# Reading a streamed weight half by even and odd partitions instead of by left and right columns

## The chip, the core and the metric

The kernel runs on one core of one Trainium2 chip. The metric is the device time of one execution in microseconds (us), and a smaller one is better. The engines are named as in the profile: PE multiplies matrices (PEld is its loading of weights), DVE, ACT and POOL work on vectors, SP issues transfers. A "q" behind an engine's name is its sequencer.

## The reference

The input x has 2048 rows of 640 numbers in bfloat16. Four layers follow each other, A, B, A, B, and each adds its result to what it gets:

```
x = x + A(layernorm(x));  x = x + B(layernorm(x))
x = x + A(layernorm(x));  x = x + B(layernorm(x))
```

A is attention over segments with a memory that goes from segment to segment. The rows are cut in 64 segments of 32. Each segment is put behind 8 memory rows, which gives 40 rows; these are projected to q, k and v for 32 heads of 192 (three matrices of 640 x 6144), attended with a mask that is causal except for the memory rows, and projected back (6144 x 640). The first 8 rows of the result are the memory of the next segment, the other 32 are the output. So the 64 segments can only be done one after the other.

B is local attention with 32 heads of 20: each row attends to itself and to the rows 2, 4, ... 14 places before it, between a projection to 1920 columns and one back to 640.

## The kernel before

One pass over the segments does all four layers. A step s handles segment s for the first A and, at the same time, segment s - 2 for the second A (LAG = 2), as two lanes l = 0 and 1 of one tile, so that each weight is used for both. It also does B for both lanes of the step before. There are 66 such steps and a last one with B alone. Each step needs the whole of the four weight matrices of A, and the new memory at its end is needed by its successor's first matmul.

**Weights.** A's weights are cut in 64 "halves" of [128 partitions, 1920 columns] bfloat16, 480 KB each: 0 to 31 for k and q (two for each pair of heads i), 32 to 47 for v, 48 to 63 for the output. 31 halves stay in SBUF (`RESIDENT`, tiles `res`). The other 33 (`STREAMED`) are read again in every step into a ring of five tiles `wt`. In step 0 a half is loaded from the matrices as they came, and POOL writes it in its SBUF form to a DRAM tile `Wr`; from step 1 on it is read from there, by two transfers on SP. `half(h)` does all this and is called by the three users of weights: `qk(i)` (L308, and L303 for i = 0), `v(i)` (L356) and `o(jh)` (L390).

**The step.** The order of a step is written out by hand in `ORDER`, four lines of words such as `q0 v0 q1 ...`. PE and SP keep exactly the order in which the program issues their instructions (`manual_schedule(engines={PE, SP})`). DVE, ACT and POOL are ordered by the scheduler of the framework, from times that it estimates, and it also puts in the waits. The last line of `ORDER` is

```
s3 pv2 wo0 o8 v13 v14 ln20 t3 v15 store0 o9 o10 pv3 o11 o12 o13 o14
```

Names that are used later, by line:

- `q` (qk): 30 matmuls `qk_ps<-ST,wt` or `res`, then ACT copies the result to `QK` (L310).
- `v`: 5 matmuls `v_ps` (L356), then a copy to `vt`, on ACT (L360) for even i and on DVE (L362) for odd i. `v15` is the last one.
- `s`, `t` (scores, p_transpose): matmuls L320 and L326, the softmax on DVE (L330 to L338) and ACT (L334, the exponential), the transpose L345, and its copies to `PT` on DVE (L347) and ACT (L348).
- `pv`: 24 matmuls `o_ps<-PT,vt` (L373), 6 for each of four `vt`; `pv3` uses v12 to v15. ACT copies the result to `ot` (L376).
- `o`: matmuls `acc<-ot,wt` or `res` (L390) that add up over the whole step in PSUM. `o14` does the halves 62 and 63.
- `finish_step`: DVE writes the new memory into `ST` of the next step (L401) and adds the residual (L414).
- B: `b_stats` (`ln10`), `b_qkv`, `b_logits`, `b_expand` (`e`), `b_wo`. Its layer norm uses POOL (L273), DVE (L275, L282 to L284, L291, L292) and ACT (L235, L236).
- `beta_x` (`ln20`): the layer norm of B's output on the same lines, but 32 columns wide; its L292 writes the second lane of the next step's `ST`.
- `input_load` and `input_tile`: every fourth step 128 new rows are loaded to `x_sb` (L241, on SP), normalised on DVE (L249 twice, L250, L252, L254) with two ACT instructions (L235, L236 on `lnst`), and transposed on PE (L259) a step later.
- `store`: every fourth step PE transposes 128 finished rows (L519) and ACT copies and stores them (L521, L522).

PSUM has six tiles (`ps`) that all these share in turn, and two more for `acc`.

Of the kernel before, what the change touches and what calls it, by code (L numbers as in the profile page):

```python
# [32 lines left out]
HALF = NCH * UW  # L33
# [73 lines left out]
class Kernel:  # L107
# [108 lines left out]
    def half(self, h):  # L216
        if h in self.resident:
            return self.resident[h]
        if h in RESIDENT:
            t = self.res.tile([P, HALF], BF16, name=f"res{h}")  # L220
            self.load_direct(t, h)
            self.resident[h] = t
            return t
        t = self.ring.tile([P, HALF], BF16, name="wt")
        if self.step == 0:
            self.load_direct(t, h)
            self.nc.gpsimd.dma_start(out=self.Wr[h][:, :], in_=t[:, :])
        else:
            for part in (slice(0, HALF // 2), slice(HALF // 2, HALF)):
                self.nc.sync.dma_start(out=t[:, part], in_=self.Wr[h][:, part])  # L230
        return t

    def rsqrt(self, var, out):
# [385 lines left out]
```

## Time and profile before

| | |
|---|---|
| time, median of 3 runs | 3518.95 us (3516.27 to 3520.65) |
| the profiled execution's own time | 3520.67 us |
| its span, first to last instruction | 3519.0 us |
| granted clock of PE, mean | 0.985 |
| PE busy | 3388.8 us, 96% |
| share of PE in the chain that ended last | 83% |
| DMA in that chain | 9% |
| read from HBM | 1091.68 MB, 316 GB/s with what is written |
| transfers `wt<-Wr` | 4290 of 240 KB, median 4.8 us from issue to landing |

A row of a group in the profile has the line, the engine, the operation, the tiles, the count, the busy time and the mean of one. A row of a wait names who waited and for whom, then the sum in us, how many times, and the longest. A row of a timeline has the start and the time taken in us, the engine, the line, the operation and its tiles, and in brackets the idle time of the engine ahead of it with what ended it. A row of a DMA queue has packets, MB and the time that its packets took, as a share of 16 engines' time. "issue" is a wait for which the profile shows no releaser.

### The profile page before, as it was taken

What the parts mean: (1) busy time and instruction counts of PE and PEld (TensorE: products, weight loads), DVE (VectorE), ACT (ScalarE), POOL (GpSimd) and SP (SyncE); (2) the same over time, 40 slices, a digit from 0 to 9 for tenths busy, and PEclk for the clock granted to TensorE, in tenths of its full rate; (3) what the DMA queues carried; (4) which work ended last, traced back from release to release, by engine and by line L of the source; (5) the groups of instructions that cost most, each with busy time, mean ns of one, the idle gap of its engine ahead of it and who ended that gap; (6) DMA issues with size and microseconds to landing.
All of it is one profiled execution on the core that took longest, in us unless ns stands there. A gap on an engine that the chain in (4) does not pass through costs nothing.

```text
span 3519.0 us, 172521 instructions
## 1 busy us (share of the span) xinstructions
PE 3388.8 (96%) x78044; PEld 2891.7 (82%) x78045; DVE 2197.2 (62%) x5056; ACT 1479.6 (42%) x3213; POOL 369.9 (11%) x467
## 2 busy tenths in 40 slices
PE   5799999999999999999999999999999999999997
PEld 3588888888888888888888888888888888888886
DVE  1366666666666666666666666666666666666665
ACT  1244444444444444444444444444444444444443
POOL 2110110010111011001101101110010111011000
PEclk7799999999999999999999999999999999999998
DMA  9999999999999999999999999999999999999995
GB/s 350 352 321 320 318 320 315 316 320 323 319 323 317 317 314 322 320 322 319 322 326 322 324 322 320 318 324 326 321 319 323 315 320 324 320 317 319 319 320 202
DMA packets 664961, 1121.84 MB, mean 319 GB/s; under 512 B 70744, under 2 KB 661472, under 8 KB 664224
## 3 DMA queue, kind: packets, MB, share of 16 engines
q1 hardware_dynamic: 659280, 1091.96, 92.5%
q0 software_dynamic: 2640, 16.22, 1.1%
q8 instruction: 610, 9.99, 1.1%
q10 hardware_dynamic: 2304, 2.62, 0.2%
q14 instruction: 127, 1.04, 0.1%
HBM read 1091.68 MB, written 18.84 MB: 316 GB/s over the span
## 4 chain that ended last, share of the span: by engine, by line
PE 83%; DMA 9%; DVE 4%; ACT 2%; SPq 1%; issue 1%; ACTq 0%; POOLq 0%; POOL 0%; DVEq 0%
PE qk_ps L308 29%; PE v_ps L356 21%; PE acc L390 13%; DMA wt<-Wr 4%; PE qkv_ps L438 4%; PE o_ps L373 3%; PE s_ps L326 3%; PE s_ps L320 3%; PE qk_ps L303 2%; PE bc_ps L480 2%; DMA x_sb<-in_A_x_dram 2%; PE pt_ps L345 1%; DMA wt<-in_A_Wv_dram 1%; SPq L214 1%; PE y_ps L492 1%
## 5 line engine op out<-in xcount | busy, mean ns | idle before, releaser
L310 ACT CAST QK<-qk_ps 128x480 bf16<-128x480 f32 x1056 | 581.5, 557 | 1042.7 <-PE qk_ps L308 828.5
L356 PE MATMUL v_ps<-wt,ST 128*128 128x384 bf16 x3630 | 717.4, 328 | 13.9 <-DMA wt<-in_A_Wv_dram 9.2
L308 PE MATMUL qk_ps<-ST,wt 128*128 128x80 bf16 x14850 | 687.8, 203 | 22.6 <-DMA wt<-in_A_Wq_dram 10.6
L308 PE MATMUL qk_ps<-ST,res 128*128 128x80 bf16 x14850 | 691.4, 202 | 18.1 <-DMA res<-in_A_Wq_dram 9.4
L308 PEld LDWEIGHTS <-wt 128*128 128x128 bf16 x14850 | 610.1, 100 | 78.8 <-DMA wt<-in_A_Wq_dram 11.8
L356 PEld LDWEIGHTS <-ST 128*128 128x128 bf16 x5280 | 466.1, 99 | 246.6 <-issue 16.4
L308 PEld LDWEIGHTS <-res 128*128 128x128 bf16 x14850 | 610.9, 100 | 48.9 <-DMA res<-in_A_Wq_dram 10.4
L390 PE MATMUL acc<-ot,res 128*128 128x80 bf16 x9900 | 465.6, 202 | 17.4 <-DMA res<-in_A_Wo_dram 9.6
L390 PEld LDWEIGHTS <-res 128*128 128x128 bf16 x9900 | 409.9, 100 | 38.3 <-DMA res<-in_A_Wo_dram 11.8
L362 DVE CAST vt<-v_ps 128x384 bf16<-128x384 f32 x528 | 290.2, 550 | 210.0 <-PE v_ps L356 209.8
L483 DVE TENSOR_TENSOR prod<-bc_ps,vh 128x512 bf16<-128x512 f32 x330 | 227.3, 689 | 245.0 <-PE bc_ps L480 244.4
L360 ACT CAST vt<-v_ps 128x384 bf16<-128x384 f32 x528 | 253.7, 481 | 244.8 <-PE v_ps L356 243.2
L485 DVE TENSOR_REDUCE oT<-prod 128x64 bf16<-128x512 bf16 x330 | 336.7, 1021 | 4.5
L356 PE MATMUL v_ps<-res,ST 128*128 128x384 bf16 x1650 | 326.8, 329 | 2.7 <-DMA res<-in_A_Wv_dram 2.7
L390 PE MATMUL acc<-ot,wt 128*128 128x80 bf16 x5940 | 309.9, 202 | 6.2 <-DMA wt<-in_A_Wo_dram 3.5
L376 ACT CAST ot<-o_ps 128x480 bf16<-128x480 f32 x528 | 268.4, 559 | 109.3 <-PE o_ps L373 109.3
L330 DVE TENSOR_TENSOR sb<-s_ps,maskA 128x320 f32<-128x320 f32 x264 | 129.7, 491 | 253.7 <-PE s_ps L326 253.6
L390 PEld LDWEIGHTS <-wt 128*128 128x128 bf16 x5940 | 261.3, 100 | 18.1 <-issue 4.7
L445 POOL TENSOR_TENSOR prod<-qT,kh 128x1280 bf16<-128x1280 bf16 x66 | 169.9, 2575 | 653.0 <-ACT kh L440 653.0
L348 ACT COPY PT<-pt_ps 64x320 bf16<-64x320 bf16 x264 | 110.9, 420 | 296.7 <-DVE PT L347 295.1
L273 POOL TENSOR_TENSOR sq<-x 128x160 f32<-128x160 bf16 x64 | 28.9, 452 | 1837.4 <-DVE x L496 1837.4
L445 DVE TENSOR_TENSOR prod<-qT,kh 128x1280 bf16<-128x1280 bf16 x66 | 201.2, 3048 | 3.4 <-ACT kh L440 3.4
(117 smaller groups left out, 3709.3 us busy)
## 6 DMA issues: line engine op xcount, KB each, us to landing
wt<-Wr SPq DMA_DIRECT2D x4290, 240.0 KB, 4.8
Wr<-wt POOLq DMA_DIRECT2D x33, 480.0 KB, 6.7
wt<-in_A_Wv_dram SPq DMA_DIRECT2D x11, 480.0 KB, 10.5
res<-in_A_Wo_dram SPq DMA_DIRECT2D x10, 480.0 KB, 10.8
wt<-in_A_Wk_dram SPq DMA_DIRECT2D x9, 480.0 KB, 11.1
res<-in_A_Wq_dram SPq DMA_DIRECT2D x9, 480.0 KB, 11.3
res<-in_A_Wk_dram SPq DMA_DIRECT2D x7, 480.0 KB, 10.2
wt<-in_A_Wq_dram SPq DMA_DIRECT2D x7, 480.0 KB, 10.2
```

What stands on the lines that cost most here:

```text
L308: nc.tensor.matmul(ps[:, m, :, :], lhsT=w[m // 3][:, c, (m % 3) * P:(m % 3 + 1) * P], rhs=st[:, c, :, 0:LT], start=(c == 0), stop=(c == NC ...
L310: nc.scalar.copy(out=self.QK[i % NQK][:, 0:12 * LT], in_=ps[:, :, :, :].rearrange("p m l t -> p (m l t)"))
L330: nc.vector.tensor_tensor(out=sb[:, :, :], in0=sv, in1=self.maskA[:, :].unsqueeze(1).to_broadcast([P, 8, LT]), op=ALU.add)
L356: nc.tensor.matmul(ps[:, :], lhsT=st[:, c, :, :].rearrange("p l t -> p (l t)"), rhs=w[:, c, :], start=(c == 0), stop=(c == NCH - 1))
L360: nc.scalar.copy(out=vt[:, :], in_=ps[:, :])
L362: nc.vector.tensor_copy(out=vt[:, :], in_=ps[:, :])
L376: nc.scalar.copy(out=ot[:, :, :, :], in_=ps[:, :, :, :, :].rearrange("p j n l t -> p (j n) l t"))
L390: nc.tensor.matmul(a[:, at, :, :], lhsT=w[h][:, m, dc * P:(dc + 1) * P], rhs=self.ots[h // 2][:, 3 * (h % 2) + m, :, :], start=(h == 0 and ...
L438: nc.tensor.matmul(ps[:, d, :, :], lhsT=self.wqkv[:, c, kind * D + d * P:kind * D + (d + 1) * P], rhs=self.xnB[:, c, :].rearrange("p (l t) ...
L445: eng.tensor_tensor(out=self.prod[:, :, l, :, :], in0=qT[:, :, l, :].unsqueeze(2).to_broadcast([P, NCH, BW, SEG]), in1=window(kh, l), op=A ...
L483: nc.vector.tensor_tensor(out=pv, in0=ps[:, :, :, :], in1=window1(self.vh, c), op=ALU.mult)
L485: nc.vector.tensor_reduce(out=self.oT[:, c, :].rearrange("p (l t) -> p l t", l=2), in_=pv.rearrange("p l w t -> p l t w"), op=ALU.add, axi ...
```

## The change

Only the two transfers of a streamed half change, from step 1 on. Before, the first one read columns 0 to 959 of all 128 partitions and the second columns 960 to 1919. After, the first one reads all 1920 columns of the partitions 0, 2, ... 126 and the second those of 1, 3, ... 127. Both forms move 240 KB per transfer, and the tiles in SBUF and in DRAM hold the same as before.

```diff
@@ -226,8 +226,8 @@
             self.load_direct(t, h)
             self.nc.gpsimd.dma_start(out=self.Wr[h][:, :], in_=t[:, :])
         else:
-            for part in (slice(0, HALF // 2), slice(HALF // 2, HALF)):
-                self.nc.sync.dma_start(out=t[:, part], in_=self.Wr[h][:, part])
+            for first in range(2):
+                self.nc.sync.dma_start(out=t[first::2, :], in_=self.Wr[h][first::2, :])
         return t
```

## The prediction

> **What bounds the kernel now.** I read the page first, then who waits for whom on PE over steps 1 to 64 (145.5 to 3438.5 us; a step lasts 51.4 us), then the end of a step on DVE, ACT and PE, and last the packets of the DMA queue.
>
> ```profile
> span 3519.0 us, 172521 instructions
> PE 3388.8 (96%) x78044; PEld 2891.7 (82%) x78045; DVE 2197.2 (62%) x5056; ACT 1479.6 (42%) x3213; POOL 369.9 (11%) x467
> ...
> q1 hardware_dynamic: 659280, 1091.96, 92.5%
> ...
> wt<-Wr SPq DMA_DIRECT2D x4290, 240.0 KB, 4.8
> ```
>
> PE is busy 96% of the span and SP's DMA queue (q1) 92.5%. Both are nearly full, so the question is which of them makes the other wait. PE's waits in steps 1 to 64 answer it:
>
> ```profile
> PE qk_ps L303 <- DVE ST L401: 14.4, 14, 1.8
> PE qk_ps L308 <- issue: 7.3, 16, 1.1
> PE acc L390 <- issue: 7.0, 8, 1.6
> PE qk_ps L308 <- DMA wt<-Wr: 6.9, 22, 0.5
> PE v_ps L356 <- issue: 3.4, 3, 1.5
> PE v_ps L356 <- DMA wt<-Wr: 1.0, 3, 0.5
> ```
>
> In 3293 us PE waits only 7.9 us (6.9 + 1.0) for streamed weights, the tile that the change touches. It waits 18.6 us for "issue" (these three lines and 0.9 in three small ones), where the profile shows no releaser, and 14.4 us for L401 on DVE. So PE sets the pace. The most that better transfers can give is 7.9 us, and 18.6 us more if the "issue" time is PE's instructions arriving late through the same full DMA engines (q8 moves 591 packets, 9.68 MB, in this stretch). That is 26.5 us, 0.75% of the time. 0.2% (7 us) is about what a measurement of this kernel can tell from no change.
>
> **The order on ACT and DVE changes too.** PE and SP are ordered by hand and POOL's order stays. On DVE and ACT the scheduler puts instructions by the times that it estimates, and in the changed program it decides otherwise at three places: the first and the third in nearly every step, the second in 14 steps.
>
> *First, DVE at the step's end, 64 steps.* The copy of v15 (L362) now stands behind L292 instead of ahead of it. DVE, then ACT, then PE before, in an ordinary step:
>
> ```profile
> 1019.22 0.31 DVE L347 COPY PT<-pt_ps 64x320 bf16<-64x320 bf16 x1
> 1019.48 0.56 DVE L362 CAST vt<-v_ps 128x384 bf16<-128x384 f32 x1
> 1020.39 0.33 DVE L292 TENSOR_TENSOR ST<-xc,ln_r 128x160 bf16<-128x160 f32 x1 [0.35 <-ACT ln_r L236]
> ```
> ```profile
> 1020.13 0.23 ACT L236 ACTIVATE ln_r<-ln_r 128x32 f32<-128x32 f32 x1
> ```
> ```profile
> 1020.47 0.62 PE L373 MATMUL o_ps<-PT,vt 128*64 128x80 bf16 x24
> ```
>
> L292 cannot start before 1020.39, since ACT's L236 releases it. The copy then starts 0.25 later (as L284 follows L291, which is as long as L292), at 1020.64, ends at 1021.20 and reaches PE 0.05 later (L401 to L303: 2205.86 to 2205.91). PE wants this vt for the last 6 of the 24 matmuls of pv3: 18 x 0.023 us after 1020.47, at 1020.88, or 0.1 earlier for its weight load. The stall is 0.37 to 0.47 us; I take 0.42. Behind it on PE stand o11 to o14 and the next step, nothing with slack. In the 16 steps with a store, PE transposes first and pv3 starts 0.34 after L292 (1071.54 against 1071.20), and o12 waits 0.3 us for ACT anyway: nothing there. So 48 x 0.42 = +20.2 us (bounds 48 x 0.30 = 14 and 48 x 0.56 = 27).
>
> *Second, DVE in the 14 steps in which an input tile arrives.* Before, all five layer-norm instructions of the tile stand ahead of L401, which makes the next step's state:
>
> ```profile
> 2203.38 0.89 DVE L249 BATCH_NORM_STATS2 bst<-x_sb 128x6 f32<-128x320 bf16 x2 [2.46 <-DMA x_sb<-in_A_x_dram]
> ...
> 2205.30 0.45 DVE L254 TENSOR_SCALAR xn<-x_sb,lnst 128x640 bf16<-128x640 bf16 x1
> 2205.66 0.20 DVE L401 CAST ST<-acc 128x48 bf16<-128x48 f32 x1
> ```
>
> L401 comes 2.28 us after x_sb has landed. After, one L249 (0.45) is left ahead of it and the others stand behind the six L401 and L414, so L401 comes 1.83 us sooner. The longest of the 14 stalls is 1.84: all of the 14.4 us goes (bound -10, if x_sb lands later). What is late next: ACT's L235 for the input now waits for L250, and q0's copy behind it moves from 1.3 to about 3.0 us after the step's start. PSUM's six tiles cover that: q0's is wanted again by q3, 5.2 us after the start.
>
> *Third, ACT.* L236 goes ahead of q2's copy (which moves by about 0.35 us), and the exponential L334 ahead of q4's copy (by 0.8 us, and qT and kh with it by 0.4 and 0.25). Those tiles are wanted over 2 us later by PE (lg at 17.2 us of the step, POOL's and DVE's products ending near 14). 0; without that cover up to 0.25 x 64 = 16 us.
>
> **The transfers.** 4290 transfers stay 4290, each 240 KB. Each had 128 rows of 1920 bytes and has 64 of 3840. Rows of 3840 bytes occur in the load of wqkv, 5 to 9 us; below it the steady stretch, 145 to 3438 us:
>
> ```profile
> q1 hardware_dynamic: 439, 1.69, 102.2%
> ```
> ```profile
> q1 hardware_dynamic: 610318, 1040.73, 94.0%
> ```
>
> 1.69 MB in 439 packets is 3840 bytes each: such a row goes as one packet, in 1.022 x 16 x 4 us / 439 = 149 ns. In the steady stretch it is 0.940 x 16 x 3293 us / 542,250 packets over 512 bytes = 91 ns for 1920 bytes. Two of those are 182 ns, so the engines' work falls by up to 18%, or not at all if a long row is stretched by a full queue as the short ones may be. The gain on PE lies between 0 and 26.5 us. I take -8, under a third, because the "issue" part is unproven and a wait is shortened rather than taken away.
>
> Two rules of the Trainium skill speak against the change. "SBUF — State Buffer", Door 1, says that a transfer's rate hangs on how many of 16 ports its partitions reach, 64 neighbouring ones reaching 8; by its formula the even partitions reach all 16. "DMA: Bandwidth & Descriptors", Rules for kernel authors, says not to split a transfer by partitions but to use all 128. No row here shows a transfer of every second partition; what halved ports would cost is a rival below.
>
> **PE's waits.** Before, a half's first weight load waits for the first transfer and a later one for the second. After, the first waits for both. An instruction carries one wait; a second is an EVENT_SEMAPHORE ahead of it. PE gets some 2145 of these (33 halves x 65 steps). Of that kind it has one per step now:
>
> ```profile
> L308 PEldq EVENT_SEMAPHORE  x65: 51/51/51, 168.3 to 3459.8; - x65
> ```
>
> One falls at 1044.78, inside a run of 30 matmuls of o that takes 1.07 us like those without it (1044.15 to 1045.22): the sequencer runs ahead, PE does not see it. 0, but where PE is already waiting for a transfer, the two matmuls that needed only the first one (2 x 0.036 us) start later: 25 waits x 0.07 = +2.
>
> **Sum.** The profiled execution took 3520.67 us. 3520.67 + 20.2 - 14.4 - 8 + 2 = 3520.5. That run lies 1.7 us over the median, 3518.95, so I say **3519 us**: no change that can be told.
>
> **Rivals.** *The copy of v15 decides (slower).* The place is pv3; it wins from the point at which the transfers give back less than 1 us: 3519 + 20.2 - 14.4 + 2 = 3527, and at 27 us for the copy 3534. For it: the order is fixed in the program and L292's release does not move. Against: the 14.4 us nearly pay for it. 0.22.
>
> *The transfers give all they can (faster).* All 26.5 us go: 3519 + 20.2 - 14.4 - 26.5 = 3498. For it: 149 against 182 ns; the stretch's DMA share of 0.96 leaves the queue little room today. Against: most of it is "issue". With half and more of it, 0.25.
>
> *PE pays for its new waits (slower).* If the 51 ns are exposed each time: 2145 x 0.051 = 109 us, 3628. Against it stand the 65 of today. 0.08.
>
> *Half the ports (slower).* If two engines share one port, a row takes 298 ns; a half's 8 rows per engine take 2.4 us, 33 of them 79 us, against the step of 51.4. The queue then sets the time: 65 x 27 us more, about 5300. 0.05. By what the Trainium skill's "SBUF — State Buffer", Door 1, says of 64 neighbouring partitions this would come; by its port formula it would not.
>
> That long rows are cut in two, so that nothing changes in the packets, is spoken against by the 439 packets; it would end in the first rival.
>
> **How the numbers follow.** No change: 0.40. Faster by over 0.2%: 0.25. Slower by over 0.2%: 0.22 + 0.08 + 0.05 = 0.35. The range reaches from the second rival (3498, and 1 for the low bound of the copy) to the first with its upper bound and the input's gain at 10 (3542): 3497 to 3542; the last two rivals are left out, 0.13, and a little at both ends.
>
> **What the profile after would show.** The packets of q1 fall by about 274,560 and its share below 92.5%. PE's waits for L401 are gone. PE or its weight load waits for DVE vt L362 at L373, about 48 times, some 0.4 us each. Waits for wt<-Wr and "issue" together fall below 26 us. EVENT_SEMAPHORE on PE counts about 2145, and runs of 30 matmuls still take 1.07 us. The prediction is wrong if L373's waits are missing (the copy has cover that I did not see), if wt<-Wr grows to several us per step (ports), or if PE's runs stretch (waits).

## The result and the profile after

The changed kernel takes **3710.78 us** (median, 3694.03 to 3725.71) against 3517.61 us before (3510.34 to 3520.65): ratio 1.0551, 95% interval 1.05 to 1.0602. It is 193 us slower; the prediction said 3519 us with a range of 3497 to 3542. The profiled execution of it took 3704.68 us. Its page:

```profile
span 3703.0 us, 174588 instructions
PE 3449.1 (93%) x78045; PEld 2916.6 (79%) x78045; DVE 2104.9 (57%) x5056; ACT 1504.4 (41%) x3213; POOL 364.8 (10%) x467
...
q1 hardware_dynamic: 384720, 1091.96, 86.8%
...
wt<-Wr SPq DMA_DIRECT2D x4290, 240.0 KB, 4.8
```

q1's packets have fallen by exactly 274,560 and its share fell from 92.5 to 86.8%: the DMA engines have more spare time than before, and still PE waits for weights. PE's waits in steps 1 to 64 (144.7 to 3621.7 us; total us, times, longest):

```profile
PE qk_ps L308 <- DMA wt<-Wr: 58.7, 75, 3.5
PE v_ps L356 <- DMA wt<-Wr: 38.3, 49, 2.2
PE qk_ps L308 <- issue: 16.3, 23, 2.0
PE acc L390 <- issue: 13.3, 17, 2.0
PE o_ps L373 <- DVE vt L362: 10.5, 42, 0.3
PE acc L390 <- DMA wt<-Wr: 7.2, 14, 1.3
```

The 64 steps take 3477.0 us instead of 3292.9, 184 more. With all lines of this view added up, waits for wt<-Wr went from 7.9 to 104.2 us, "issue" from 18.6 to 41.0, L401 from 14.4 to 0.7; L373's wait for the copy of v15 is new. Together PE's waits went from 42 to 168 us. Another 57 us stand in PE's busy time (3248 us before, 3305 after, in these steps). Much of that goes with the waits too: in a run a matmul starts every 0.036 us, but the last one ahead of a wait counts with its whole 0.2 us, and there are 259 waits where there were 72; that is 34 us. The weight loads (PEld) wait for the streamed tile as well, 57 times and 61 us, but 51 of these fall in time in which PE stands, and are counted above.

What has changed ahead of all this is SP. Its issue of one transfer, in ns min/median/max, in the kernel before and after:

```profile
L230 SPq DMA_DIRECT2D wt<-Wr x4290: 319/400/2304, 134.3 to 3482.7; - x195
```
```profile
L230 SPq DMA_DIRECT2D wt<-Wr x4290: 450/587/2552, 133.5 to 3666.9; - x195
```

And SP itself waits much longer for the output store, after and, below it, before:

```profile
SPq L230 <- DMA out_dram<-yo: 71.8, 15, 6.1
```
```profile
SPq L230 <- DMA out_dram<-yo: 4.2, 8, 0.9
```

**The slot's way round.** Each streamed half goes into one of five slots. For the 2046 halves of steps 2 to 63 the traces give the mean time of each leg: from the last matmul that read the slot's old half to the issue of the first new transfer; from there to the second transfer's issue (part of the next leg); from the first issue to the later landing; from there to the first matmul that reads it; the reading itself. The sum is what one slot takes for one half; times 33 halves over 5 slots it is the step. In us:

| kernel | free to issue | (1st to 2nd issue) | issue to landed | landed to use | use | step |
|---|---|---|---|---|---|---|
| before | 0.195 | (0.449) | 5.425 | 1.341 | 0.832 | 51.4 |
| after | 0.522 | (0.614) | 5.580 | 1.290 | 0.833 | 54.3 |

After, a slot waits 0.33 us longer for SP, and the half lands 0.155 us later. 0.48 x 33/5 x 64 = 203 us; the leg from landing to use is 0.05 us shorter, which takes back 21 us. The legs add up to the step by their definition, so this says where the time stands and not yet why.

### The profile page after: what moved, and what is told of

The parts are those of the page before. It is cut to its first block, busy times and chain, and to the rows that moved or that the text cites. A ratio compares the mean times of both kernels' runs of the same rounds, so it can differ in the third digit from the quotient of the medians.

```text
span 3703.0 us, 174588 instructions
## 1 busy us (share of the span) xinstructions
PE 3449.1 (93%) x78045; PEld 2916.6 (79%) x78045; DVE 2104.9 (57%) x5056; ACT 1504.4 (41%) x3213; POOL 364.8 (10%) x467
## 3 DMA queue, kind: packets, MB, share of 16 engines
q1 hardware_dynamic: 384720, 1091.96, 86.8%
## 4 chain that ended last, share of the span: by engine, by line
PE 67%; DMA 19%; DVE 7%; SPq 3%; issue 2%; ACT 2%; POOLq 0%; POOL 0%; ACTq 0%; DVEq 0%
PE qk_ps L308 23%; DMA wt<-Wr 16%; PE v_ps L356 16%; PE acc L390 12%; PE qkv_ps L438 3%; PE o_ps L373 2%; PE s_ps L326 2%; PE s_ps L320 2%; SPq L230 2%; PE qk_ps L303 2%; DMA wt<-in_A_Wv_dram 2%; PE bc_ps L480 2%; DVE vt L362 1%; PE pt_ps L345 1%; SPq L214 1%
## 5 line engine op out<-in xcount | busy, mean ns | idle before, releaser
L310 ACT CAST QK<-qk_ps 128x480 bf16<-128x480 f32 x1056 | 583.8, 555 | 1027.0 <-PE qk_ps L308 838.8
L308 PE MATMUL qk_ps<-ST,wt 128*128 128x80 bf16 x14850 | 699.0, 203 | 83.1 <-DMA wt<-Wr 58.7
L356 PE MATMUL v_ps<-wt,ST 128*128 128x384 bf16 x3630 | 718.8, 329 | 52.3 <-DMA wt<-Wr 38.8
L308 PEld LDWEIGHTS <-wt 128*128 128x128 bf16 x14850 | 616.3, 101 | 150.0 <-issue 65.3
L308 PE MATMUL qk_ps<-ST,res 128*128 128x80 bf16 x14850 | 694.4, 203 | 24.7 <-DMA res<-in_A_Wk_dram 8.4
L356 PEld LDWEIGHTS <-ST 128*128 128x128 bf16 x5280 | 465.9, 99 | 296.3 <-issue 51.6
L308 PEld LDWEIGHTS <-res 128*128 128x128 bf16 x14850 | 613.2, 101 | 56.9 <-DMA res<-in_A_Wk_dram 10.7
L390 PE MATMUL acc<-ot,res 128*128 128x80 bf16 x9900 | 467.0, 203 | 19.1 <-issue 11.2
L390 PEld LDWEIGHTS <-res 128*128 128x128 bf16 x9900 | 410.9, 100 | 40.0 <-issue 13.1
L356 PE MATMUL v_ps<-res,ST 128*128 128x384 bf16 x1650 | 328.7, 330 | 4.0 <-DMA res<-in_A_Wv_dram 2.3
L390 PE MATMUL acc<-ot,wt 128*128 128x80 bf16 x5940 | 309.2, 202 | 17.1 <-DMA wt<-Wr 7.2
L390 PEld LDWEIGHTS <-wt 128*128 128x128 bf16 x5940 | 258.7, 100 | 33.9 <-issue 16.2
L445 POOL TENSOR_TENSOR prod<-qT,kh 128x1280 bf16<-128x1280 bf16 x66 | 191.1, 2895 | 745.3 <-ACT kh L440 745.3
L334 ACT ACTIVATE sb<-sb 128x320 f32<-128x320 f32 x264 | 124.1, 470 | 192.2 <-DVE sb L333 192.0
```

What stands on the lines that cost most here:

```text
L308: nc.tensor.matmul(ps[:, m, :, :], lhsT=w[m // 3][:, c, (m % 3) * P:(m % 3 + 1) * P], rhs=st[:, c, :, 0:LT], start=(c == 0), stop=(c == NC ...
L310: nc.scalar.copy(out=self.QK[i % NQK][:, 0:12 * LT], in_=ps[:, :, :, :].rearrange("p m l t -> p (m l t)"))
L334: nc.scalar.activation(out=sb[:, :, :], in_=sb[:, :, :], func=ACT.Exp, scale=SCA)
L356: nc.tensor.matmul(ps[:, :], lhsT=st[:, c, :, :].rearrange("p l t -> p (l t)"), rhs=w[:, c, :], start=(c == 0), stop=(c == NCH - 1))
L390: nc.tensor.matmul(a[:, at, :, :], lhsT=w[h][:, m, dc * P:(dc + 1) * P], rhs=self.ots[h // 2][:, 3 * (h % 2) + m, :, :], start=(h == 0 and ...
L445: eng.tensor_tensor(out=self.prod[:, :, l, :, :], in0=qT[:, :, l, :].unsqueeze(2).to_broadcast([P, NCH, BW, SEG]), in1=window(kh, l), op=A ...
```

## The experiments

All ratios are to the kernel before, run on the same chip, where it took 3517 to 3522 us beside each experiment. First the transfer's form, with everything else as before.

**Partitions 0-63 and 64-127.** 
```
-            for part in (slice(0, HALF // 2), slice(HALF // 2, HALF)):
-                self.nc.sync.dma_start(out=t[:, part], in_=self.Wr[h][:, part])
+            for part in (slice(0, P // 2), slice(P // 2, P)):
+                self.nc.sync.dma_start(out=t[part, :], in_=self.Wr[h][part, :])
```


> Two transfers of whole rows again, but partitions 0-63 and 64-127 instead of even and odd; the order of instructions on DVE, ACT, POOL and SP is that of before, so neither the copy of v15 nor the 14 input steps play a part, and none of the lanes moves. PE's first weight load of a half still waits for both transfers. Four theories stand for the 186-193 us that the change cost. ISSUE (SP needs 450/587 ns, min/median, for a transfer of every second partition against 319/400, so slots are refilled later): here it depends on what makes the issue long; if it is the step over partitions, SP shows about 320/400 and the time is within 20 us of before; if it is the 64 rows of 3840 bytes, SP shows 450/587 and the time is 3518 + 100 to 140. FIRST WAIT (the first weight load needs both transfers): slower than before by 60 us or more with SP at 320/400. STORE (SP waits 72 us for the output store in 15 steps) and ORDER (copy of v15, +16 to 20): same as before, as neither is in this kernel. If engines share ports by partitions, the queue's share goes to 100% and the time to thousands of us more (5300 by the rival in the prediction).

Measured: 4692.97 us, 1.3323 (1.3285 to 1.3361). Its SP line and its queue:

```profile
L230 SPq DMA_DIRECT2D wt<-Wr x4290: 444/445/2135, 134.1 to 4656.2; - x195
```
```profile
q1 hardware_dynamic: 384720, 1091.96, 99.5%
```

The same 384,720 packets fill the queue: they cost 0.995 x 4692.7 / (0.868 x 3703.0) = 1.45 times the engine time of even and odd partitions. So the dearer packets, which the prediction held possible for the change itself as a sharing of ports, come with neighbouring partitions and not with every second one. The Trainium skill, "SBUF — State Buffer", Door 1, draws that line by its port formula, and these two shares agree with it. The long issue (444 ns at the least) is here too: it belongs to 64 partitions, not to the step of two.

**Column halves, second columns first.** 
```
-            for part in (slice(0, HALF // 2), slice(HALF // 2, HALF)):
+            for part in (slice(HALF // 2, HALF), slice(0, HALF // 2)):
```


> The two column halves of before (128 rows of 1920 bytes each), the second columns asked for first. Orders on all engines are those of before, SP's issue costs are those of before (319/400 ns). PE's first weight load now needs the transfer that is issued last, as after the change. FIRST WAIT: this alone makes PE late, 60 us or more over before, and wt<-Wr among PE's waits rises from 8 to over 60 us. ISSUE, STORE and ORDER: within 15 us of before, since a late half costs PE only the two or three matmuls that it could have run ahead (0.07 us for qk, 0.18 for o, 0.33 for v, where PE is waiting at all).

Measured: 3529.67 us, 1.0038 (1.0024 to 1.0051). PE's wait for both transfers costs 8 to 18 us by itself, far from 60.

**One transfer for each half.** 
```
+            w = self.Wr[h]
+            self.nc.sync.dma_start(out=t[:, :], in_=w[:, :])
```


> One transfer of 128 rows of 3840 bytes for each half; orders on DVE and ACT as before. SP issues 2145 transfers instead of 4290. ISSUE: SP's time for issues falls (one issue for each half, even at 600 ns it is 20 us a step against 31 before and 40 after), a half is complete earlier by one issue, so PE's waits for wt<-Wr stay near 8 us and the time is 3490 to 3525. FIRST WAIT: the first weight load waits for the whole half as after the change, so slower than before by 60 us or more. STORE, ORDER: as before.

Measured: 3604.91 us, 1.0243 (1.0225 to 1.026). Both expectations missed the way of it. SP's issue takes 319/320 ns, slots are refilled at once (0.03 us), but PE stands 67 us for "issue" (18.6 before) and only 15.5 for wt. Every one of its 54 "issue" gaps over 0.4 us ends 1.1 to 1.6 us after a 16 KB packet of the instruction queue (q8) has ended, where the mean distance of such packets is 5.7 us. I read this as PE's next instructions coming late through the same DMA engines. The Trainium skill, "DMA: Bandwidth & Descriptors", Rules for kernel authors, advises one transfer over 128 partitions in place of two partition halves. It is faster here than even and odd partitions (3605 against 3711), but two column halves are faster than both.

**The output store off SP's semaphores.** The edit is on the changed kernel:
```
-        nc.scalar.dma_start(out=self.out[...], in_=yo[:, :])
+        nc.gpsimd.dma_start(out=self.out[...], in_=yo[:, :])
```


> The changed kernel with one edit: POOL issues the output store instead of ACT, so that no transfer of SP follows it in its lane. Orders on DVE and ACT are those of the changed kernel. STORE: SP's 72 us of waits for out_dram vanish, the 15 steps that showed 56.5 us against 53.5 of their neighbours come down to 53.5, and the time falls by 40 to 50 us, to 3660-3670. ISSUE, FIRST WAIT, ORDER: what SP waits there is taken from waits that it would have had anyway, and the time stays within 10 us of the changed kernel's 3711.

Measured: 3657.98 us, 1.0407 (1.0374 to 1.044): 53 us come back. Why it costs so much shows in the trace of the changed kernel. The hardware transfers of SP and ACT take eight completion semaphores in turn, and a transfer waits for the one before it on its own. At 1115.39 us ACT issues the store, and SP's next transfer is the one behind it on that semaphore (ACT's and SP's instructions):

```profile
1115.39 0.34 ACTq L522 DMA_DIRECT2D out_dram<-yo  x1
```
```profile
1120.10 0.45 SPq L230 DMA_DIRECT2D wt<-Wr  x1
```

SP stands 4.7 us from the store's issue until it has landed, and the DMA engines run dry (their busy tenths, and GB/s, in 40 slices of 1115 to 1121 us):

```profile
DMA  7888999897966768997654331000000000300000
GB/s 307 358 333 358 333 333 333 333 333 307 365 256 256 282 265 316 367 376 256 273 205 171 128 111 60 34 26 17 17 26 9 0 0 0 109 0 0 0 0 0
```

It is so at all 15 stores of steps 1 to 64: the semaphore's next user is SP's first transfer behind the store. Before, it is the seventh, and SP waits 4.2 us for stores in all. The step after each store lasted 56.5 us in the changed kernel and lasts 53.6 here, as its neighbours do.

**Short rows again.** Both kernels get a gap of 64 bytes in DRAM between a row's column halves:
```
-            self.Wr = {h: self.dram.tile([P, HALF], ...
+            self.Wr = {h: self.dram.tile([P, 2, HALF // 2 + 32], ...
```


> The changed kernel with the cached weights laid out in DRAM with a gap of 64 bytes between the two column halves of a row, so that even and odd partitions still go as two transfers, but in packets of 1920 bytes (128 for each transfer) as before the change. Orders on all engines are those of the changed kernel. LONG ROWS (rows of 3840 bytes keep the DMA engines from PE's instruction fetches and cost the time that single transfers lost, 86 us): PE's waits for issue fall from 36 to 20 us or less and the time falls by 20 to 60 us, to 3650-3690. ISSUE (SP's time for a transfer of 64 partitions): no change within 15 us if SP shows 450/587 again; more if SP needs longer for 128 packets than for 64; if SP's time follows the form of the rows and comes out at 320/400, then back to 3580 or below.

> The single transfer for each half again (3605 us), with the same gap in DRAM, so that its 256 packets have 1920 bytes. Orders on DVE and ACT are those of before. LONG ROWS: PE's waits for issue fall from about 70 us to the 18 to 25 of before, and the time to 3520-3540. If it is the size of the transfer (480 KB in one go ahead of everything else) and not the length of its rows, it stays within 15 us of 3605.

Measured: 3707.0 us, 1.0535 (1.0515 to 1.0554), the same as the changed kernel; and 3580.06 us, 1.0167 (1.0151 to 1.0182), 25 below the single transfer but still 1.7% above before. So shorter rows by themselves gave the changed kernel nothing back. SP's line of the two:

```profile
L230 SPq DMA_DIRECT2D wt<-Wr x4290: 579/597/2287, 134.7 to 3665.9; - x195
```
```profile
L230 SPq DMA_DIRECT2D wt<-Wr x2145: 517/518/1659, 134.7 to 3541.1; - x195
```

Two packets to a row make the issue longer still, which muddies both: in the first, slots wait 0.69 us for SP, so that a gain from shorter rows could hide behind it.

**The scheduler's order, in the kernel before.** The copy of v15 behind L292; the input tile's layer norm behind the step's end:
```
+        elif i == 15 and 1 <= self.step <= self.n_seg:
+            with self.tc.issue_after(self.applied):      # L292
+                nc.vector.tensor_copy(out=vt[:, :], in_=ps[:, :])
```


> The kernel before with one thing pinned: the copy of v15 stands behind L292 on DVE in every step, as in the changed kernel; nothing else moves on any engine. ORDER (first term of the prediction): +20 us (14 to 27), 3533 to 3545. If pv3 has cover that the prediction did not see: within 5 us of before. If the ring of five slots takes the delay back (SP refills while PE stands): less than half, +2 to +10.

```
+                        with tc.issue_after(self.last_xr):   # the last L414
                             self.input_tile(s // 4 + 1)
```


> The kernel before with one thing pinned: the input tile's layer-norm instructions stand behind L401 and L414 of the step's end on DVE in the 14 steps that take an input tile; some ACT instructions move with them. Second term of the prediction: the 14.4 us of L401's stalls go, 3500 to 3508. If the time is set by the ring (slot released to landed) rather than by PE's own work, PE stands elsewhere instead and the gain is under 7 us.

Measured: 3537.34 us, 1.005 (1.0037 to 1.0063), +18; and 3510.49 us, 0.9974 (0.996 to 0.9987), -9. PE's wait of the first (lines stand three further down in this kernel):

```profile
PE o_ps L376 <- DVE vt L363: 13.1, 48, 0.3
```

48 times, as the prediction counted, but 0.27 us each where it had 0.42. In the second, waits for L401 are gone.

**SP busier, first try.** Four and eight empty instructions on SP behind each transfer of the kernel before:

```
                 self.nc.sync.dma_start(out=t[:, part], in_=self.Wr[h][:, part])
+                for _ in range(4):                           # or 8
+                    self.nc.sync.nop(nofuse=True)
```


> The kernel before with four empty instructions on SP behind each streamed transfer, so that SP is busy longer with each as it is after the change (147 ns more on the mean there: 40.4 against 30.7 us for the 66 transfers of a step). Rows, packets and all orders are those of before. How long four of them take will be read from the distance of SP's two transfers of a half (0.45 us on the mean before, 0.61 after the change); between 70 and 200 ns are possible. ISSUE: slower, in proportion; the two runs that showed the other parts leave 3711 - 3518 - 53 (store) - 17 (order) + 10 (input) - 12 (first wait) = about 120 us for 147 ns, so at that length 3600 to 3640, at 70 ns 3555 to 3575. If SP's time is hidden (it waits for slots 20 us of each step): within 10 us of before.

> The same with eight empty instructions: ISSUE says twice the loss of the run with four or more, since a busier SP has more slots waiting in line; hidden says nothing until SP is full, at 66 x 0.78 us = 51.4 us a step, which eight would only reach at 40 ns each.

Measured: 0.9994 (0.9981 to 1.0008) and 1.0003 (0.9992 to 1.0014). They say nothing: the instructions did not come to execution, SP has its 6581 instructions and the distance of 0.44 us as before.

**The changed kernel with store and order put right.** On top of the store on POOL, L292 is pinned behind the copy of v15 (excerpt):

```
-        self.ln_apply(self.x2_next[:, :, :], m, r, ...)      # L291 and L292 ahead of v15's copy
+        nc.vector.tensor_tensor(out=self.xc2[:, :, :], ...)  # L291 stays
+    def apply(self):                                         # a stage of its own, behind v15
+        with self.tc.issue_after(self.v15):
+            self.nc.vector.tensor_tensor(out=self.ST[...][:, :, 1, NM:LT], in0=self.xc2[:, :, :], ...)
```


> The changed kernel with the store issued by POOL (3658) and, besides, the copy of v15 pinned ahead of L292 on DVE, as it is before the change. ORDER: PE's 43 waits at L373 for vt go, and the time falls by the 16 us that the same order cost in the kernel before, to 3637-3647. If the ring sets the time in this kernel (a slot's release to its landing), PE's wait only moves into waits for wt: within 7 us of 3658.

Measured: 3650.09 us, 1.0381 (1.0357 to 1.0405). 8 us less than with the store alone, with intervals that overlap: not told apart. What it leaves is 3650 - 3530 = 120 us over the swapped column halves, with the copy of v15 in the same place and the same wait for both transfers. The input tile still stands behind the step's end here, which is worth 9 us, so the form of the transfers costs nearer 129.

**A slightly better kernel.** Before, with two of the edits above together (`issue_after(self.last_xr)` around the input tile, `nc.gpsimd.dma_start` for the store):

> The kernel before with the input tile's layer norm behind the step's end on DVE (3510) and the store issued by POOL. STORE as a fault of the changed kernel's timing alone: before waits only 4.2 us for out_dram, so 3505 to 3512. If the store on a lane of SP costs every kernel its waits: 3460 to 3490.

Measured: 3507.56 us, 0.997 (0.9958 to 0.9982): the input's gain, and nothing for the store. The store costs only where its place on the semaphores falls badly.

**SP busier, in earnest.** Semaphore increments, which do execute, behind each transfer of the kernel before (three, six), and three with the swapped columns:
```
                 self.nc.sync.dma_start(out=t[:, part], in_=self.Wr[h][:, part])
+                for _ in range(3):
+                    self.nc.sync.sem_inc(self.busy)
```


> The kernel before with three increments of an unused semaphore on SP behind each streamed transfer; rows, packets and all orders are those of before. One such instruction and the gap to the next take about 50 ns on SP by the traces (17 and some 33), so the distance of a half's two transfers goes from 0.45 to about 0.60 us, against 0.61 after the change. ISSUE: most of the 120 us that are open, 3590 to 3640. HIDDEN (SP waits for slots for 20 us of each step): within 15 us of before, and the 120 us belong to the form of the transfers (64 partitions of long rows), not to SP's time.

> The same with six increments: distance about 0.75 us, and SP busy for 66 x 0.75 = 49.5 us of a step of 51.4 by itself. ISSUE: more than twice the loss of the run with three, 3700 or over. HIDDEN: 3520 to 3600.

> Column halves with the second columns asked for first (3530 by itself) and three increments on SP behind each transfer: PE's first weight load needs the later transfer, and SP is as busy as after the change, with rows of 1920 bytes over 128 partitions. If SP's time and the wait for both transfers are all that is left of the change: as the changed kernel with store and order put right (3650), 3630 to 3665. If the form of the transfers has a cost of its own beside SP's time: clearly under that, 3530 to 3600.

Measured: 3518.91 us, 1.0008 (0.9993 to 1.0024); 3795.83 us, 1.0792 (1.0764 to 1.0821); 3527.86 us, 1.003 (1.0014 to 1.0046). With three, the distance of a half's transfers is 0.616 us, as after the change, and it costs nothing. Only at 0.80 us (six), where SP waits 288 us for PE to free a slot and not 1194 as before, does the time rise. My theory, that SP's greater load by itself is the missing 120 us, falls. The transfers' own issue shows what these runs left out (three increments):

```profile
L230 SPq DMA_DIRECT2D wt<-Wr x4290: 319/320/2577, 134.2 to 3482.0; - x195
```

An increment behind a transfer keeps SP busy while the transfer is already under way. A longer issue does not: from the end of its issue a transfer's last landing takes 4.37 us before, 4.26 after, 4.27 with three increments (means over the transfers whose landing the profile tells). And where the transfer queue had run empty, the first packet starts 0.78 to 0.80 us after the end of the issue in the changed kernel (issue 0.45 us) as in the one with short rows (0.58 us). So the transfer's start follows the end of its issue.

**The delay ahead of the transfer.** Swapped columns; an empty instruction takes the wait for the slot, and increments stand between it and the transfer:
```
+                self.nc.sync.clobber_nop([self.nc.sync.lower_ap(t[:, part])])
+                for _ in range(2 if part.start else 1):
+                    self.nc.sync.sem_inc(self.busy)
                 self.nc.sync.dma_start(out=t[:, part], in_=self.Wr[h][:, part])
```


> Column halves of 128 partitions with the second columns asked for first (3530 by itself, 3528 with three increments behind each transfer). Now an empty instruction of SP takes the wait for the slot, and increments stand between it and the transfer: two for the first transfer of a half, one and a second small wait for the second. By 50 to 62 ns each the first transfer starts 0.15 to 0.19 us after its slot is free and the second 0.62 to 0.65 us after the first, as if each issue were as long as after the change; rows, packets, the partitions and the orders on DVE and SP are those of before. OWN ISSUE (the transfer begins when its issue ends, so a longer issue makes each landing later): most of what separates 3528 from the changed kernel with store and order put right (3650): 3590 to 3660. FORM (something else in transfers of every second partition): within 20 us of 3530.

Measured: 3572.7 us, 1.0156 (1.0134 to 1.0177). 45 us over the run with three increments behind each transfer: a delay ahead of it does cost, but neither theory's range holds the result. The legs say which part is which:

| kernel | free to issue | (1st to 2nd issue) | issue to landed | landed to use | use | step |
|---|---|---|---|---|---|---|
| swapped | 0.174 | (0.437) | 5.377 | 1.443 | 0.827 | 51.6 |
| swapped, three behind | 0.351 | (0.614) | 5.339 | 1.304 | 0.823 | 51.6 |
| swapped, delay ahead | 0.756 | (0.609) | 5.233 | 1.079 | 0.822 | 52.1 |
| after, store and order right | 0.383 | (0.613) | 5.636 | 1.205 | 0.832 | 53.2 |

The delay came out longer than meant (at least 0.297 us from the free slot to the issue, against 0.030). By it, a half is in its slot 0.756 + 5.233 = 5.99 us after the slot was free, nearly as late as in the changed kernel with store and order right (0.383 + 5.636 = 6.02). So the lateness of the transfers is reproduced on the mean, and 45 us is what it costs. The other 3650 - 3573 = 77 us lie mostly after the landing: 1.205 against 1.079 us to first use. There PE waits 48.6 us for "issue" against 6.7, 5.9 against 0.7 for ACT's copies of QK, and 62.9 against 44.8 for wt. The largest "issue" row of each, of the changed kernel with store and order right and then of the run with the delay ahead (whose lines stand three further down):

```profile
PE qk_ps L308 <- issue: 21.2, 32, 1.8
```
```profile
PE qk_ps L311 <- issue: 3.5, 4, 1.4
```

The name "issue" does not catch all of it. Of the waits for wt over 0.4 us, 25 of 62 in the first and 15 of 47 in the second end 1.1 to 1.65 us behind a 16 KB packet of q8 too, where chance would give a tenth. Whatever the profile names as their end, 80 waits with 69 us stand at that place in the changed kernel with store and order right, 24 with 20 us in the run with the delay ahead, and 23 with 17 us before.

## Why the prediction was wrong, step by step

**The step that failed is the transfers** ("4290 transfers stay 4290 ... The gain on PE lies between 0 and 26.5 us"). The count was right and the price of issuing one was left out: the row for it stood in the trace of before (319/400 ns), and the new form was taken to cost the same. It costs 147 ns more on the mean (40.4 us of issues in a step for 66 transfers, against 30.7). The floor of zero had no reason behind it: the change could only gain, in that sum, because only the DMA engines were priced. In place of -8 us the form of the transfers cost 120 to 129. The later transfers account for 45 of these, as the delay ahead of them shows; for the rest the cause stays open.

**The price of a long packet** came from wqkv's load (149 ns). In the steady stretch the queue's row of after is

```profile
q1 hardware_dynamic: 339908, 1040.57, 88.0%
```

Less the 68,068 packets up to 512 bytes that before also had there (610,318 - 542,250), 0.880 x 16 x 3477 us / 271,840 = 180 ns, where two short ones were 182. The prediction's other end, "not at all", was the right one.

**The store** was in no term. The prediction took "PE and SP are ordered by hand" as the end of the matter; SP's order did stay, but the transfer that shares the store's semaphore became its very next one: 53 us, the largest single cause shown.

**PE's waits**: the EVENT_SEMAPHOREs are there, 2146 of them (L303 66, L308 975, L356 715, L390 390), and cost nothing that can be seen, as said: a run of 30 matmuls takes 1.07 us in the median, as before. The wait for both transfers was put at 2 us and is 12 (8 to 18): it was counted from the 25 waits of before. That a later half meets more of them is likely, but not shown.

**The copy of v15**: 48 waits and 18 us in the kernel before, against 20.2 forecast (14 to 27). Right in the count and the sum; the waits that the profile shows are shorter than forecast and add up to 13 us. **The input tile**: 9 us against 14.4 (the interval reaches from 5 to 14); right in its mechanism. **ACT's order**: put at 0; PE waits 4.5 us for L310 after, and for none of it before.

**The rivals.** Half the ports was rightly kept off the even partitions; for neighbouring partitions, where that rival's rise in price did come, a packet costs 1.45 times as much and not twice, so 4693 and not 5300 us. PE paying 51 ns each time did not come. The copy of v15, the first rival, came with its price, but that is a tenth of the loss, and the gain of the second did not come at all. No rival had SP in it. Of the signs, wt and "issue" together were to stay under 26 us and came to 145.

**The range** does not follow from its own terms: the second rival with the low bound of the copy gives 3498 - 6 = 3492 and not 3497, the first with its upper bound and the input's gain at 10 gives 3534 + 4 = 3538 and not 3542. Neither makes a difference to the outcome.

**The account of the 193 us:** store 53; copy of v15 between 8 (changed kernel) and 18 (kernel before); input -9; wait for both transfers 12; lateness of the transfers 45; the rest, 74 to 84 us, shows mostly after the landing, about half of it as PE's "issue" (+42 us against the run with the delay ahead). That these gaps are late instruction packets is read from the trace and not tested (in the changed kernel the 42 gaps over 0.4 us all end 1.1 to 1.6 us after one); why transfers of 64 partitions should hold them up more than column halves at the same distance stays open. Short rows, with 3707 us and 38 us of "issue", speak against the length of the rows, as far as their longer issue lets them, and no run here separates the partitions from their issue time.

## What to carry to other kernels

Price a transfer on the engine that issues it as well as on the queue: in a ring of slots a transfer starts when its issue ends, so nanoseconds of issue lengthen every slot's way round, while work that stands behind a transfer is free until the issuing engine is full. When a change lets the scheduler place a transfer elsewhere, look up which transfer comes next on its semaphore, even on another engine. A delay is best tested at the place where it arises: increments behind the transfers cost nothing, and nearly the same distance between two transfers (0.61 us) cost 45 us when the delay stood ahead of them.

## What was not expected of the hardware

- SP's issue of one transfer takes, at the least, 319 ns for 128 rows of one packet (1920 or 3840 bytes alike), 517 for 128 rows of two, 444 to 450 for 64 rows of one and 579 for 64 rows of two: half the rows take longer, not shorter.
- With a single transfer of 480 KB PE's waits for "issue" are 67 us (48 with short packets) where two column halves, 0.45 us apart, leave 18.6; with 0.62 us between them they are 10.7, but with two transfers of 64 partitions, 0.61 us apart, 41. With 0.80 us the profile names none, yet 92 of PE's 147 waits for wt over 0.4 us then end 1.1 to 1.65 us behind a packet of the instruction queue: an empty "issue" row does not show that these packets came in time.
- 64 neighbouring partitions raise the engines' time for the same packets 1.45 times, every second partition not at all (180 ns for 3840 bytes, against 182 for two packets of 1920 before).
